# Two FNet and two H3 layers on one core: 16-point groups and rows handed out in three steps, late rows in one region, X sums from an earlier step

## The chip, the core and the metric

The kernel runs on one core of one Trainium2 chip. A core has TensorE (PE, matrix products, with its weight loads shown as PEld), VectorE (DVE), ScalarE (ACT), GpSimd (POOL) and SyncE (SP, which issues most of the transfers). Each engine works through its own queue of instructions in order and waits at an instruction until what that instruction needs is there. The metric is the device time of one execution in microseconds. The kernel before has a median of 1230.15 us over 3 runs (1229.99 to 1231.23).

## What is computed

Two kinds of layer alternate on an array x of 2048 positions and 576 channels, float32 throughout:

```python
x = A_x
x = x + _A_ref(_layernorm(x, axis=-1), A_dft_seq_re, A_dft_seq_im, A_dft_hid_re, A_dft_hid_im)
x = x + _B_ref(_layernorm(x, axis=-1), B_k, B_v, B_shift_k, B_ssm_k, B_ssm_D)
x = x + _A_ref(_layernorm(x, axis=-1), A_dft_seq_re, A_dft_seq_im, A_dft_hid_re, A_dft_hid_im)
x = x + _B_ref(_layernorm(x, axis=-1), B_k, B_v, B_shift_k, B_ssm_k, B_ssm_D)
return x
```

`_A_ref` multiplies by a hidden transform (576 by 576) and a sequence transform (2048 by 2048), both complex, and keeps the real part. `_B_ref(q, k, v, ...)` is q times y, where y is a long convolution (over 2048 positions, for each channel) of kv, and kv is a 4-tap convolution of k times v. k and v are inputs, so y does not depend on x: it is one array, the same for both B layers, and only the gating q * y depends on x.

## The kernel before

**Precision.** Every float32 operand is split into a high part (rounded for fp32r) and a low part: `split(h, l, src)` is an ACT copy (L86) and a DVE subtraction (L87). A product is three matmuls, high by high, high by low, low by high. All matmuls are recorded at L69.

**Rows.** Positions are stored as 16 rows (tiles) of 128 positions, x[:, j, :]; `xs` holds the normalised rows, split. `to_x` (L172 to L178) writes a row there.

**Layer 1 (first A layer).** `layer` (L278) goes through 128 steps n: 4 blocks of 512 output positions (tb), real and imaginary part (g), 16 rows (k). A step loads a c tile of 128 by 512 (`load_c`, two steps ahead; raw tile in the ring `craw`, its split form in the ring `cs`) and does 14 matmuls of 512 columns into four banks s0 to s3 and rm. It yields twice: after half of the sequence matmuls (whole is False) and at its end (whole is True). At the end of a block's part the banks are emptied (`evac_u`, `evac_r`), and four `hidden` products (L254: 54 matmuls of 288 columns each, in two pieces) are put on the list `pending`, to be handed out by `finish` between steps. They use W, the split hidden matrices, loaded by `load_w` (L203) at steps 41 to 43, three chunks each.

**The branch.** y of the B layers is computed beside layer 1 by the generator `branch` (L325): a 128-point transform (`f1_products`, steps up to 40), then 64 groups of 16-point products (`mid_forward`, `mid_inverse`), then the inverse 128-point products (`i2_products`, 32). The main loop (L614 to L646) asks it for its next part whenever a step's share of the time is used up: each part says how much it is worth by what it yields (L508, L514, L524), and `paced` gives each step's share. A group loads a tile of t (`load_feed`, two groups ahead), splits it (`split_feed`, one group ahead), multiplies it (`mid_forward`: two halves of three matmuls each, the kernel half into bank pk, emptied by four ACT copies L434 to L437, and the signal half into px, multiplied by these on DVE, L439 to L441), and two groups later goes back (`mid_inverse`: three matmuls, emptied by L453). All of these, and `hidden`, take their banks in turn from three (`bank`, named bk).

**The gate and layer 2.** `get_x1` (L574) makes row j of the second A layer's input: it loads the first layer's output xa and y's row yb, normalises and gates (`gated`, L526: statistics on DVE, the power on POOL, two passes on DVE), stores xb, normalises again (`normed_x`, L534: two ACT passes with sums, the power on POOL, a third ACT pass), stores the result to y_d and writes it to `xs`. Rows 0 to 7 are made at every second step from step 113 of layer 1 on, rows 8 to 15 at the steps of layer 2 listed in `ROWS`. Their buffers xa and yb are rings of six, two in the tile `flts` and four in the tile `gate`. Layer 2's first block runs 32 steps of `layer`; its sums go out by `save_u` (L708) and `store_r` (L713). At step `STATIC` the regions are laid out anew: rings csum and cw come into `flts`, the tile `ph` into the region that `gate` had. `build_load` (L662) reads pairs of normalised rows back, `build` (L671) forms their sums and differences (four of them, four parts each) for the other three blocks, which `strassen` (L784) computes with seven products in place of eight; its steps load c tiles of twice the size (`raw_c`).

**Order.** The program is written in this order, but each engine's queue is ordered by a scheduler, by its estimate of when an instruction is ready: the trace shows instructions ahead of ones that precede them in the program (L672 of `build`, handed out at step 20, ahead of L717 of step 15). `tc.issue_after(ins)` puts what a block issues on the engine of `ins` behind it; `load_after` keeps SP's loads behind the last c load (`anchor`), `load_fr` those of POOL behind the last power.

Of the kernel before, what the change touches and what calls it, by code (L numbers as in the profile page):

```python
# [27 lines left out]
ROWS = (0, 1, 2, 3, 4, 5, 7, 9)  # L28
# [4 lines left out]
W_SAVE = 60  # L33
I2_END = 111
# [13 lines left out]
STATIC = 14  # L48
B_LOAD = 15
B_FROM = 20  # L50
# [9 lines left out]
def fnet_h3_kernel(ctx: ExitStack, tc: tile.TileContext, x, c_mat, w_re, w_im, k_pad, v, shift_k,  # L60
# [82 lines left out]
    anchor, stored, pows = [], [], []  # L143
# [22 lines left out]
    def normed(src, y):  # L166
        mv, rs, nb = norm_stats(src)
        yield
        nc.vector.tensor_scalar(nb, mv[:, 0:1], rs, -1.0, op0=OP.mult, op1=OP.mult)
        nc.scalar.activation(y, src, AF.Identity, bias=nb, scale=rs)  # L170
# [154 lines left out]
    def branch():  # L325
# [101 lines left out]
        def mid_forward(df):  # L427
            pk, px = bank(), bank()
            for ps, o in ((pk, HD), (px, 0)):
                mm(ps[:, :HD], mc[:, 0, :], df[0][:, o:o + HD], True, False)  # L430
                mm(ps[:, :HD], mc[:, 0, :], df[1][:, o:o + HD], False, False)
                mm(ps[:, :HD], mc[:, 1, :], df[0][:, o:o + HD], False, True)
            kk = two(ring["kk"]())
# [3 lines left out]
            nc.scalar.activation(kk[hi, 1, :], pk[hi, :HD], AF.Copy, scale=-1.0)  # L437
            p1, p2 = kk[:, 0, :], ring["p2"]()
# [62 lines left out]
        for i, (kind, hf, q) in enumerate(feeds):  # L501
# [3 lines left out]
            else:  # L505
# [3 lines left out]
                yfs.append((hf, q, mid_forward(df)))  # L509
# [14 lines left out]
            yield I2_COST if kind else 2.7  # L524

    def gated(xa, j, late=False):  # L526
        mv, rs, _ = norm_stats(xa)
        q = ring["yb"]()
        (load_after if late else nc.sync.dma_start)(q, yb_d[j])
        nc.vector.scalar_tensor_tensor(q, xa, mv[:, 0:1], q, op0=OP.subtract, op1=OP.mult)  # L530
        nc.vector.scalar_tensor_tensor(q, q, rs, xa, op0=OP.mult, op1=OP.add)
        return q

    def normed_x(src, y, junk):  # L534
# [6 lines left out]
        pows.append(nc.gpsimd.tensor_tensor(rs, sv, mhalf, OP.pow).ins)  # L541
        yield
# [16 lines left out]
    def get_x0(j):  # L559
        if X[j] is None:  # L560
            load_x(j + 2)
# [10 lines left out]
    ready = set()  # L572

    def get_x1(j):  # L574
        if j in ready:
            return
        ready.add(j)
        xa = ring["xa"]()
        load_after(xa, xa_d[j])
        xb = gated(xa, j, True)  # L580
        nc.sync.dma_start(xb_d[j], xb)
        y = xa
        for _ in normed_x(xb, y, ring["xj"]()):
            pass
# [29 lines left out]
    for n, whole in layer(get_x0, lambda j: x[:, j, :], done0, pending):  # L614
# [7 lines left out]
        if whole and F1_END < n <= W_END:  # L622
            for _ in range(3):
                next(wl, 0)
            if n == W_END - 1:
                next(br)
# [340 lines left out]
```

## Time and profile before

| what | value |
|---|---|
| median of 3 runs | 1230.15 us (1229.99 to 1231.23) |
| the profiled execution | 1229.91 us |
| its span, first to last instruction | 1228.0 us |
| mean granted TensorE clock | 0.991 |
| DMA | 261.96 MB, mean 213 GB/s |
| shares of the chain that ended last | PE 76%, DVE 7%, DMA 7%, ACT 5%, issue 3% |

How to read it: a line of the busy table gives an engine's busy time, its share of the span and its count of instructions. A row of a timeline gives start, length, engine, line, operation, the tiles written and read, the shape, how many in a row, and in brackets how long the engine stood idle before and what ended that. SPq and ACTq rows are transfers being issued. A row of waits gives who waited for whom, the total, how often, and the longest. The granted clock is the share of full speed that the throttle allowed TensorE.

### The profile page before, as it was taken

The page shows a single profiled execution, that of the slowest core. Times are in us where ns is not written, and L with a number is a line of the kernel's source. Part 1 is how long each engine was busy: PE and PEld are TensorE (multiplying, and loading weights), DVE is VectorE, ACT ScalarE, POOL GpSimd, SP SyncE. Part 2 cuts the span into 40 slices and gives each one's busy share as a digit, 9 for nine tenths or more (in the row PEclk, how much of TensorE's full clock was granted, in tenths as well). Part 3 has the DMA queues.
Part 4 walks back from the last instruction along what each step waited for, and adds up shares of the span by engine and source line. Part 5 has one row for each costly group of instructions (what it writes and reads, how often), then busy time and mean ns, then how long its engine had stood idle before and what let it go on. Part 6 is the DMA issues. An engine that isn't in the chain of part 4 may idle for free.

```text
span 1228.0 us, 18406 instructions
## 1 busy us (share of the span) xinstructions
PE 1189.8 (97%) x6320; PEld 1032.7 (84%) x6320; DVE 849.3 (69%) x1559; ACT 657.3 (54%) x1315; POOL 85.5 (7%) x116
## 2 busy tenths in 40 slices
PE   7999999999999999999999899899999999999997
PEld 5778888887878888888988798788888888889997
DVE  7999982849787567675346864675766767774674
ACT  7855664749776577775445653534444445550210
POOL 2310000000000000000111221000000000000111
PEclk9999999899999999999999899999999999999999
DMA  8889988736655656655976764973474477795631
GB/s 296 302 246 300 313 240 246 218 99 169 210 188 187 220 169 186 202 170 177 316 216 229 259 239 139 282 248 122 130 276 153 145 279 256 248 326 162 214 118 39
DMA packets 145967, 261.96 MB, mean 213 GB/s; under 512 B 15825, under 2 KB 44497, under 8 KB 145874
## 3 DMA queue, kind: packets, MB, share of 16 engines
q1 hardware_dynamic: 102674, 205.73, 52.3%
q10 hardware_dynamic: 36288, 42.48, 9.9%
q0 software_dynamic: 6912, 12.59, 4.1%
q8 instruction: 49, 0.80, 0.3%
q14 instruction: 44, 0.36, 0.1%
HBM read 194.09 MB, written 66.65 MB: 212 GB/s over the span
## 4 chain that ended last, share of the span: by engine, by line
PE 76%; DVE 7%; DMA 7%; ACT 5%; issue 3%; POOL 1%; SPq 0%; ACTq 0%; POOLq 0%; DVEq 0%
PE s L69 41%; PE bk L69 31%; PE rm L69 4%; DVE mats L87 1%; DMA flts<-in_c_mat 1%; DMA f1f<-in_k_pad 1%; DMA gate<-xa 1%; POOL flts L541 1%; ACT mats L86 1%; DMA flts<-in_w_re 1%; ACT flts L436 1%; DVE u L87 1%; DVE flts L160 1%; DMA flts<-t 1%; ACT mid L86 0%
## 5 line engine op out<-in xcount | busy, mean ns | idle before, releaser
L69 PE MATMUL s<-mats 128*128 128x512 f32 x2094 | 530.9, 394 | 11.5 <-DVE u L87 7.7
L69 PEld LDWEIGHTS s<-mats 128*128 128x128 f32 x2094 | 386.3, 189 | 88.0 <-DVE u L87 8.6
L86 ACT ACTIVATE mats<-flts 128x512 fp32r<-128x512 f32 x202 | 126.2, 626 | 106.0 <-PE rm L69 53.8
L87 DVE TENSOR_TENSOR mats<-flts,mats 128x512 fp32r<-128x512 f32 x202 | 138.3, 687 | 53.4 <-ACT mats L86 51.9
L69 PE MATMUL bk<-mid 128*128 128x288 f32 x768 | 128.9, 302 | 7.2 <-ACT mid L86 4.1
L69 PEld LDWEIGHTS bk<-mid 128*128 128x128 f32 x768 | 113.8, 189 | 25.5 <-ACT mid L86 8.4
L87 DVE TENSOR_TENSOR mid<-flts,mid 128x576 fp32r<-128x576 f32 (+1 forms) x160 | 100.5, 637 | 34.9 <-ACT mid L86 29.4
L69 PE MATMUL bk<-w,u 128*128 128x288 f32 x864 | 122.5, 299 | 1.2 <-ACT flts L453 1.2
L69 PEld LDWEIGHTS bk<-w,u 128*128 128x128 f32 x864 | 119.9, 191 | 4.6 <-ACT flts L453 1.6
L86 ACT ACTIVATE mid<-flts 128x576 fp32r<-128x576 f32 (+1 forms) x160 | 92.4, 586 | 37.6 <-DVE flts L442 27.8
L69 PE MATMUL rm<-mats 128*128 128x512 f32 x308 | 96.1, 391 | 3.3 <-DVE flts L717 2.5
L163 POOL TENSOR_TENSOR flts<-flts 128x1 f32<-128x1 f32 x40 | 36.8, 921 | 527.6 <-DVE flts L162 527.6
L69 PEld LDWEIGHTS rm<-mats 128*128 128x128 f32 x308 | 57.5, 188 | 16.3 <-DVE flts L717 2.9
L69 PE MATMUL bk<-f1r 128*128 128x288 f32 x384 | 59.8, 300 | 7.6 <-ACT f1r L86 6.5
L69 PEld LDWEIGHTS bk<-f1r 128*128 128x128 f32 x384 | 56.6, 192 | 11.7 <-ACT f1r L86 6.5
L69 PE MATMUL bk<-mats 128*128 128x288 f32 (+1 forms) x370 | 66.0, 316 | 0.0
L69 PE MATMUL s<-t,mats 128*128 128x512 f32 x258 | 65.6, 396 | 0.0
L265 DVE TENSOR_TENSOR flts<-flts,bk 128x288 f32<-128x288 f32 x48 | 21.6, 451 | 59.3 <-PE bk L69 59.2
L69 PEld LDWEIGHTS s<-t,mats 128*128 128x128 f32 x258 | 49.3, 191 | 10.5
L69 PE MATMUL bk<-mats,t 128*128 128x288 f32 (+1 forms) x362 | 57.4, 302 | 0.0
L69 PEld LDWEIGHTS bk<-mats 128*128 128x128 f32 x370 | 54.4, 188 | 3.2
L399 ACT ACTIVATE flts<-bk 128x288 f32<-128x288 f32 x128 | 48.3, 408 | 14.2 <-PE bk L69 12.2
(145 smaller groups left out, 1542.0 us busy)
## 6 DMA issues: line engine op xcount, KB each, us to landing
flts<-in_c_mat SPq DMA_DIRECT2D x149, 256.0 KB, 3.5
ph<-in_c_mat SPq DMA_DIRECT2D x54, 512.0 KB, 4.6
t<-flts ACTq DMA_DIRECT2D x64, 288.0 KB, 5.0
flts<-t SPq DMA_DIRECT2D x64, 288.0 KB, 3.6
flts<-in_c_mat SPq DMA_DIRECT2D x30, 512.0 KB, 5.0
vd<-flts ACTq DMA_DIRECT2D x64, 144.0 KB, 3.1
flts<-vd SPq DMA_DIRECT2D x32, 288.0 KB, 4.6
mid<-in_i2c POOLq DMA_DIRECT2D x32, 256.0 KB, 4.4
```

The source lines that it names most:

```text
L69: nc.tensor.matmul(ps, lhsT, rhs, start=first, stop=last, skip_group_check=more)
L86: nc.scalar.activation(h, src, AF.Copy)
L87: nc.vector.tensor_tensor(l, src, h.bitcast(F32), OP.subtract)
L160: nc.vector.bn_stats(st[:, i, :], src[:, i * HD:(i + 1) * HD])
L163: pows.append(nc.gpsimd.tensor_tensor(rs, ve, mhalf, OP.pow).ins)
L265: nc.vector.tensor_tensor(r[:, cs], r[:, cs], ps[:, :HD], OP.add)
L399: nc.scalar.activation(so[:, c, :], ps[:, :HD], AF.Copy)
L436: nc.scalar.activation(kk[lo, 1, :], pk[hi, :HD], AF.Copy)
L541: pows.append(nc.gpsimd.tensor_tensor(rs, sv, mhalf, OP.pow).ins)
```

## The change

- `mid_forward` becomes `mid_kernel` (kernel half and its four copies) and `mid_signal` (signal half and what follows). The branch yields 1.6 between them and 1.1 at the end, where it yielded 2.7 at the end.
- The branch's groups are set up at step 44 in place of 42 and handed out from step 45 in place of 44 (`MID_FROM`).
- `get_x1` becomes the generator `make_x1` in three parts: loads and first statistics; gating, store, second sums; normalising, store and split. `advance` moves every row in the making on by one part at each step and starts a new one where there is one. In odd rows the first statistics are sums on ACT (`sums`, two passes over the row) in place of bn_stats on DVE. The load of yb stands ahead of the statistics, also in `done1`.
- Late rows: `ROWS` ends in 6, 8 in place of 7, 9; from step 0 of layer 2 on xa and yb are rings of four, in `gate` alone.
- `STATIC` is step 11 in place of 14. The first `build_load` is at step 12 in place of 15. The parts of `build` are handed out from step 16, one at even and two at odd steps, in place of two at each step from 20 on.
- At the start, row 0's statistics and normalisation come ahead of the first two c tiles in the program, and the DVE instructions of these two are tied behind the row's bias (`biased`); the load of x tile 2 follows the second c tile, as it did.

```diff
 XLEAD = 3
-ROWS = (0, 1, 2, 3, 4, 5, 7, 9)
+ROWS = (0, 1, 2, 3, 4, 5, 6, 8)
 K_FIRST = 2
...
 W_SAVE = 60
+MID_FROM = 45
 I2_END = 111
...
 STAT = 20
-STATIC = 14
-B_LOAD = 15
-B_FROM = 20
+STATIC = 11
+B_FROM = 16
 X_RING = 8
...
-    anchor, stored, pows = [], [], []
+    anchor, stored, pows, biased = [], [], [], []
...
         yield
-        nc.vector.tensor_scalar(nb, mv[:, 0:1], rs, -1.0, op0=OP.mult, op1=OP.mult)
+        biased.append(nc.vector.tensor_scalar(nb, mv[:, 0:1], rs, -1.0, op0=OP.mult, op1=OP.mult).ins)
         nc.scalar.activation(y, src, AF.Identity, bias=nb, scale=rs)
...
-        def mid_forward(df):
-            pk, px = bank(), bank()
-            for ps, o in ((pk, HD), (px, 0)):
-                mm(ps[:, :HD], mc[:, 0, :], df[0][:, o:o + HD], True, False)
-                mm(ps[:, :HD], mc[:, 0, :], df[1][:, o:o + HD], False, False)
-                mm(ps[:, :HD], mc[:, 1, :], df[0][:, o:o + HD], False, True)
-            kk = two(ring["kk"]())
+        def mid_half(df, o):
+            ps = bank()
+            mm(ps[:, :HD], mc[:, 0, :], df[0][:, o:o + HD], True, False)
+            mm(ps[:, :HD], mc[:, 0, :], df[1][:, o:o + HD], False, False)
+            mm(ps[:, :HD], mc[:, 1, :], df[0][:, o:o + HD], False, True)
+            return ps
+        def mid_kernel(df):
+            pk, kk = mid_half(df, HD), two(ring["kk"]())
             nc.scalar.activation(kk[lo, 0, :], pk[lo, :HD], AF.Copy)
...
             nc.scalar.activation(kk[hi, 1, :], pk[hi, :HD], AF.Copy, scale=-1.0)
+            return kk
+        def mid_signal(df, kk):
+            px = mid_half(df, 0)
             p1, p2 = kk[:, 0, :], ring["p2"]()
...
                     yield 0.4
-                yfs.append((hf, q, mid_forward(df)))
+                kk = mid_kernel(df)
+                yield 1.6
+                yfs.append((hf, q, mid_signal(df, kk)))
             split_feed(i + 1)
...
                 load_feed(i + 4)
-            yield I2_COST if kind else 2.7
-
-    def gated(xa, j, late=False):
-        mv, rs, _ = norm_stats(xa)
-        q = ring["yb"]()
-        (load_after if late else nc.sync.dma_start)(q, yb_d[j])
-        nc.vector.scalar_tensor_tensor(q, xa, mv[:, 0:1], q, op0=OP.subtract, op1=OP.mult)
-        nc.vector.scalar_tensor_tensor(q, q, rs, xa, op0=OP.mult, op1=OP.add)
-        return q
-
-    def normed_x(src, y, junk):
+            yield I2_COST if kind else 1.1
+    def sums(src, junk):
         m = ring["stat"]()
...
         pows.append(nc.gpsimd.tensor_tensor(rs, sv, mhalf, OP.pow).ins)
+        return sm, rs, nb
+    def gated(xa, q, j, junk=None):
+        load_after(q, yb_d[j])
+        if junk is None:
+            mv, rs, _ = norm_stats(xa)
+            mean, op = mv[:, 0:1], OP.subtract
+        else:
+            mean, rs, _ = sums(xa, junk)
+            op = OP.add
+        yield
+        nc.vector.scalar_tensor_tensor(q, xa, mean, q, op0=op, op1=OP.mult)
+        nc.vector.scalar_tensor_tensor(q, q, rs, xa, op0=OP.mult, op1=OP.add)
+    def normed_x(src, y, junk):
+        sm, rs, nb = sums(src, junk)
         yield
...
         if X[j] is None:
-            load_x(j + 2)
+            if j > 0:
+                load_x(j + 2)
             stats0(j)
...
-    ready = set()
+    def make_x1(j):
+        xa, q = ring["xa"](), ring["yb"]()
+        load_after(xa, xa_d[j])
+        for _ in gated(xa, q, j, ring["xj"]() if j % 2 else None):
+            yield
+        nc.sync.dma_start(xb_d[j], q)
+        for _ in normed_x(q, xa, ring["xj"]()):
+            yield
+        stored.append(nc.sync.dma_start(y_d[j // 2][:, j % 2, :], xa).ins)
+        X[j] = to_x(xa, j)
+        ready.add(j)
+    ready, making = set(), []
+    def advance(j=None):
+        for row in list(making):
+            if next(row, 0) == 0:
+                making.remove(row)
+        if j is not None:
+            making.append(make_x1(j))
+            next(making[-1])
     def get_x1(j):
-        if j in ready:
-            return
-        ready.add(j)
-        xa = ring["xa"]()
-        load_after(xa, xa_d[j])
-        xb = gated(xa, j, True)
-        nc.sync.dma_start(xb_d[j], xb)
-        y = xa
-        for _ in normed_x(xb, y, ring["xj"]()):
+        assert j in ready
+    def done1(j, xa):
+        q = ring["yb"]()
+        for _ in gated(xa, q, j):
             pass
-        stored.append(nc.sync.dma_start(y_d[j // 2][:, j % 2, :], y).ins)
-        X[j] = to_x(y, j)
-
-    def done1(j, xa):
-        nc.sync.dma_start(out[:, j, :], gated(xa, j, True))
+        nc.sync.dma_start(out[:, j, :], q)
...
     next(br)
-    load_c((0, 0, 0))
-    load_x(1)
-    load_c((0, 0, 1))
     get_x0(0)
+    with tc.issue_after(biased[0]):
+        load_c((0, 0, 0))
+        load_x(1)
+        load_c((0, 0, 1))
+        load_x(2)
     next(br)
...
-    for n in range(W_END + 1, I2_END + 1):
+    for n in range(MID_FROM, I2_END + 1):
         total += STEP + PIECE * pieces(n)
...
                 next(wl, 0)
-            if n == W_END - 1:
-                next(br)
+        if whole and n == MID_FROM - 1:
+            next(br)
         if n > W_END:
...
                 finish(pending, 1)
-            m = n - W_END - 1
-            if m + 1 < len(paced):
+            m = n - MID_FROM
+            if m < 0:
+                done_by = -1.0
+            elif m + 1 < len(paced):
                 done_by = paced[m] + (paced[m + 1] - paced[m] if whole else STEP * 3 / 7)
...
             lay(flts, SC_AT + CRAW * NT + 2 * D, ("xa", D, 2), ("yb", D, 2))
-            lay(region_b(F32, "gate"), 0, ("xa", D, 4), ("yb", D, 4), ("xj", D, 2))
-        if m >= 0 and m % 2 == 0:
-            get_x1(m // 2)
+            gate = region_b(F32, "gate")
+            lay(gate, 0, ("xa", D, 4), ("yb", D, 4), ("xj", D, 2))
+        if m >= 0:
+            advance(None if m % 2 else m // 2)
     T, R, t7 = {}, {}, []
...
         finish(pending, 1)
-        if n in ROWS:
-            get_x1(J // 2 + ROWS.index(n))
+        if n == 0:
+            fresh("xa", "yb")
+            lay(gate, 0, ("xa", D, 4), ("yb", D, 4))
+        advance(J // 2 + ROWS.index(n) if n in ROWS else None)
         if n == STATIC:
...
             ring["cs"].tiles.extend([free, *held])
-        if n >= B_FROM:
-            if (n - B_FROM) % 2 == 0 and len(builds) < KP:
+        if n == STATIC + 1:
+            loaded.append(build_load(0))
+        for _ in range(1 + n % 2 if n >= B_FROM else 0):
+            if next(builds[-1], 0) == 0 if builds else True:
+                if len(builds) == KP:
+                    break
                 builds.append(build(len(builds), *loaded[len(builds)]))
-            next(builds[-1], None)
-            next(builds[-1], None)
-        if n == B_LOAD or n >= B_FROM and (n - B_FROM) % 2 == 0 and len(loaded) < KP:
-            loaded.append(build_load(len(loaded)))
+                next(builds[-1])
+                if len(loaded) < KP:
+                    loaded.append(build_load(len(loaded)))
         if n >= 30:
...
```

## The prediction, made before the changed kernel was run

> **What bounds the kernel now.** I read the head of the page first, then a table of busy time by stage, then the timelines round the stretches where TensorE's column falls short. From the page:
>
> ```profile
> span 1228.0 us, 18406 instructions
> PE 1189.8 (97%) x6320; PEld 1032.7 (84%) x6320; DVE 849.3 (69%) x1559; ACT 657.3 (54%) x1315; POOL 85.5 (7%) x116
> ```
>
> The busy table by stage (stretch, length, busy time and count of PE, weight load, DVE, ACT, POOL, granted clock, DMA share, GB/s):
>
> ```profile
> 200.00:225.00 25.00, 21.59 (x104) 19.02 (x104) 12.93 (x20) 14.32 (x26) 1.58 (x3) 0.86 0.91 289
> 225.00:575.00 350.00, 343.75 (x1936) 299.65 (x1935) 250.57 (x493) 247.39 (x546) 6.75 (x13) 1.00 0.58 178
> 675.00:700.00 25.00, 20.70 (x81) 16.67 (x80) 20.04 (x51) 16.69 (x33) 5.53 (x7) 0.86 0.79 269
> 775.00:800.00 25.00, 21.80 (x87) 16.91 (x86) 19.12 (x35) 13.86 (x26) 0.00 (x0) 0.93 0.93 293
> ```
>
> TensorE sets the time; a change that leaves its matmuls alone can win only its holes. Idle PE (length less busy) is 3.4, 6.3, 4.3 and 3.2 us in these rows, 17.2 of the 38.2 in all (1228.0 less 1189.8); of the rest, the change reaches only the part in term 1. A hole also costs clock: 0.86 over 25 us is 7.0 us at half speed, a loss of 3.5 us on top of the idle; 0.93 is 1.75 us more.
>
> In the stage of the 16-point groups (225 to 575) idle time is not the whole loss. The steady pace is read from two undisturbed pieces of the chain of waits, the work from the groups by shape inside that stretch:
>
> ```profile
> 804.64 2.72 PE s L69 x12
> 1105.63 115.02 PE bk L69 x866
> ```
>
> ```profile
> L69 PE MATMUL s<-mats 128*128 128x512 f32 x697 | 181.9, 393 | 1.6 <-DVE u L87 1.6
> L69 PE MATMUL bk<-mid 128*128 128x288 f32 x636 | 107.8, 301 | 3.8 <-ACT flts L437 1.1 <-ACT flts L453 1.0 <-ACT mid L86 0.7
> L69 PE MATMUL bk<-w,u 128*128 128x288 f32 x487 | 67.0, 295 | 0.0
> L69 PE MATMUL rm<-mats 128*128 128x512 f32 x116 | 36.5, 392 | 0.8 <-ACT flts L464 0.8
> ```
>
> A 512-column matmul takes 2.72/12 = 0.227 us, a 288-column one 115.02/866 = 0.133. (697+116) x 0.227 + (636+487) x 0.133 = 333.9 us, so 16.1 us of the 350 are lost here, the largest sum of any stage, in many small pieces.
>
> **The change part by part.** No matmul is added or removed. The price of each edit is what it does to one hole.
>
> **1. First row's bias first.** The timeline of the start:
>
> ```profile
> 5.10 0.55 POOL L163 TENSOR_TENSOR flts<-flts 128x1 f32<-128x1 f32 x1 [4.66 <-DVE flts L162]
> 6.43 0.76 DVE L87 TENSOR_TENSOR f1r<-f1f,f1r 128x576 fp32r<-128x576 f32 x1 [1.41 <-ACT f1r L86]
> 7.97 0.69 DVE L87 TENSOR_TENSOR mats<-flts,mats 128x512 fp32r<-128x512 f32 x1 [0.77 <-ACT mats L86]
> 9.31 0.20 DVE L169 TENSOR_SCALAR flts<-flts 128x1 f32<-128x1 f32 x1
> 11.33 3.00 PE L69 MATMUL s<-mats 128*128 128x512 f32 x12 [1.55 <-ACT mats L174]
> ```
>
> The bias (L169) could run from 5.65, when the power is done, but stood behind a split of a c tile (7.97). Tied ahead of it, it runs at 7.19 at the latest (behind L87 of 6.43), 2.1 us sooner; the row is then ready before the earlier matmuls end, at 11.33 - 1.55 = 9.8. At most 1.6 us are won. The second row, still as late, is needed next, so I take **1.0**, bounds -0.5 (the c split now waits for the bias) to 1.6. The order of the loads on SP stays: x tile 2 stood behind the second c tile before, too.
>
> **2. The groups start one step later (42/44 to 44/45).** TensorE and SP around the hole:
>
> ```profile
> 212.65 0.39 PE L69 MATMUL s<-mats 128*128 128x512 f32 x1
> 216.45 0.85 PE L69 MATMUL bk<-mid 128*128 128x288 f32 x2 [3.41 <-ACT mid L86]
> ```
>
> ```profile
> 212.35 0.90 SPq L147 DMA_DIRECT2D flts<-t  x2
> 215.65 0.57 SPq L212 DMA_DIRECT2D flts<-in_w_re  x1
> ```
>
> After one matmul of step 44 TensorE waits for the first group, whose two t loads stand in the SP queue among the nine W loads. Later, those loads go behind W, and 13 more matmuls of step 44 (13 x 0.227 = 2.95 us) come before a group is due: they fill nearly all of the 3.41, and the 3.5 of clock goes with it, 6.4 at most. Next late is W: its last tile is issued at 215.65, and the first hidden-size product would now start at 212.65 + 3.2 = 215.9 and want its ninth tile 24 x 0.133 = 3.2 us later, at 219.1. The first group, loaded by the row of 212.35, was ready at 216.45, 4.1 us after its issue; by that measure W's last tile is ready at 219.8, and its split takes its turn behind eight others. The two t loads of 288 KB that no longer stand ahead of it (2 us at the row's 289 GB/s) make up for part of this, so some 2 us of wait and part of the clock may come back. I take **3.0**, bounds -1.5 (t loads now too late: one step's lead instead of two) to 6.4.
>
> **3. Groups in three steps.** A group's nine matmuls were handed out as inverse (3) and forward (6); now inverse, kernel half, signal half, with pauses 0.4 / 1.6 / 1.1 in place of 0.4 / 2.7. What their weight loads waited for between 225 and 575:
>
> ```profile
> PEld bk L69 <- ACT mid L86: 4.4, 11, 0.8
> PEld bk L69 <- ACT flts L437: 4.3, 9, 0.7
> PEld bk L69 <- ACT flts L453: 2.8, 6, 1.2
> PEld bk L69 <- DVE flts L441: 1.4, 4, 0.5
> ```
>
> L437, L453 and L441 empty banks: 8.5 us. With a pause between kernel and signal, the four copies of the kernel half lie under sequence matmuls, and the signal's bank is written only when its factor is ready, so it is held for a shorter time. I take half, **4.0**. L86 (data of the next group late) is untouched or worse, see the rivals. Bounds: the 16.1 of the stage less the hole of the u eviction (1.6) and rm (0.8) that no group causes leaves 13.7; below, -4.4, the L86 row's wait once more. The 64 more changes between kinds of matmul add no instruction.
>
> **4. Rows of layer 2 in three steps; odd rows' first sums on ACT.** DVE and ACT before the hole at 690:
>
> ```profile
> 686.85 0.81 DVE L160 BATCH_NORM_STATS2 flts<-flts 128x6 f32<-128x288 f32 x2
> 688.01 0.81 DVE L530 SCALAR_TENSOR_TENSOR flts<-flts 128x576 f32<-128x576 f32 x1
> 690.06 0.15 DVE L540 TENSOR_SCALAR flts<-flts 128x1 f32<-128x1 f32 x1
> 692.36 0.57 ACT L86 ACTIVATE u<-s 128x512 fp32r<-128x512 f32 x1
> 693.84 1.65 PE L69 MATMUL s<-mats 128*128 128x512 f32 x3 [4.21 <-DVE u L87]
> 688.17 0.76 ACT L539 ACTIVATE gate<-flts 128x576 f32<-128x576 f32 x1
> ```
>
> The layer's first matmul waits for the eviction of s (ACT at 692.36), queued behind row 6's chain, whose L540 (690.06) stands behind row 7's statistics and gating on DVE (from 686.85 on). If only the statistics of row 7, now on ACT, go (0.81 and two short operations), L540 comes about 1.1 us sooner; if its gating (two of 0.81) too falls behind the eviction, 2.7, and with a hole of 1.5 the 3.5 of clock falls too: 6.2. But row 7's operations were brought ahead of an eviction that precedes them in the program, and nothing in the change forbids that; and its two new passes on ACT (0.76 each by the row of L539) may land ahead of the eviction. I take **2.5**, bounds -1.5 to 6.2. Loading q ahead of the statistics in the last rows lies under their matmuls.
>
> **5. Late rows in one region, STATIC 14 to 11, X sums from 16.** The hole near 781 and what precedes it:
>
> ```profile
> 754.33 2.88 PE L69 MATMUL s<-mats 128*128 128x512 f32 x12
> 755.17 0.45 DVE L265 TENSOR_TENSOR flts<-flts,bk 128x288 f32<-128x288 f32 x1
> 768.14 0.33 SPq L585 DMA_DIRECT2D y<-gate  x1
> 768.51 1.20 SPq L147 DMA_DIRECT2D flts<-in_c_mat  x2
> 770.20 2.88 PE L69 MATMUL s<-mats 128*128 128x512 f32 x12
> 771.20 0.63 ACT L86 ACTIVATE t<-flts 128x512 fp32r<-128x512 f32 x1 [1.48 <-DMA flts<-in_c_mat]
> 782.16 0.29 DVE L672 TENSOR_TENSOR flts<-flts 128x128 f32<-128x128 f32 x1 [1.00 <-DMA flts<-y]
> 783.88 0.74 PE L69 MATMUL rm<-mats 128*128 128x512 f32 x2 [2.49 <-DVE flts L717]
> ```
>
> rm waits for store_r's L717, behind X sums (L672) that wait for their y loads. Those loads move from step 15 to 12, about 9.5 us (3 x 3.17, a step from 770.20 - 754.33 over five), and the late rows no longer sit in the flts part that they fill. The sums are then due before the eviction: 2.49 + 1.75 of clock, 4.2 at most. I take **3.5**. Against it: c tiles from step 14 on are now queued on SP behind row 15's store (768.14) and step 14 starts at 770.20; a c tile issued at 768.51 was split from 771.20, plus 0.63: step 14 would stand 1.6 us, with 1.75 of clock 3.4, the lower bound -3.4. Row 15's chain can start up to 3 us sooner (its product ended before 754.33, its L265 came at 755.17, in a DVE queue blocked by row 14's chain), which would hide this.
>
> The Trainium skill ("TensorE: Matmul & The Clock Gate", section "HAM oscillation — how this bites in real kernels") warns only of idle gaps above about 3.4 us; the 2.49 gap here was followed by a clock of 0.93. By that rule term 5 would be 1.75 less than by the row and my sum 1.75 less; the measured clock decides.
>
> **Sum**: 1.0 + 3.0 + 4.0 + 2.5 + 3.5 = 14.0 us off the profiled execution of 1229.91 us (span 1228.0 and 1.9 round it; 0.24 below the median of the runs): **1215.9**. The bounds add to -0.5 - 1.5 - 4.4 - 1.5 - 3.4 = -11.3 (1241.2) and 1.6 + 6.4 + 13.7 + 6.2 + 4.2 = 32.1 (1197.8).
>
> **The rivals.** *A, slower: the next group's data.* split_feed follows the signal half, so its lead on the next kernel half shrinks from 2.7 + 0.4 to 1.1 + 0.4 of a group's 3.1 units, from a full group to half of one, about 2.5 us (350 us over 64 groups and 12 later products is 4.6 us each). The split is an ACT and a DVE pass behind the signal's own operations. It decides once the split ends after its turn on TensorE; at 0.4 us for each of 64 groups it costs 25.6 in place of the gain of 4.0: 1229.9 - 10.0 + 25.6 = 1245.5; at 0.2 us, 1232.7. For it: the L86 row is already the longest. Against: ACT is busy 247 and DVE 251 of 350 us, and the split needs only its load, so it may be brought forward. *B, less: only the late rows act*, and the pace of the groups shifts waits from bank to bank: 1229.9 - 2.5 - 3.5 = 1223.9. *C, more: each hole closes* but for half of the third term's upper bound: 1229.9 - 1.6 - 6.4 - 6.9 - 6.2 - 4.2 = 1204.6. *D, no effect*: each queue is ordered anew, and holes closed open elsewhere: about 1229.
>
> **How the numbers follow.** Forecast (1208 to 1222) 0.48, B (1222 to 1227.7) 0.17, C (below 1208) 0.15, D (within 0.2%, 2.5 us, about what a measurement of this kernel can tell) 0.06, A (above 1232.6) 0.14. Faster is 0.48 + 0.17 + 0.15 = 0.80. The range 1204 to 1232 leaves out half of C and A: about 2 in 10.
>
> **What would show it.** Right: the first sequence matmul by 10; clock 1.00 in 200-225; lost time in the groups' stage near 12 us by the same count; no wait of rm for L717. Wrong: more weight loads waiting for L86 (A); a stall at step 14 of layer 2 with c tiles behind row 15's store; the eviction of s at the layer change still behind row 7 (term 4 nil).

## The result, and the profile after

| kernel | median, us (range, runs) | ratio to before, 95% interval |
|---|---|---|
| before | 1230.15 (1227.54 to 1231.23, 5) | |
| changed | 1237.06 (1235.47 to 1242.35, 5) | 1.0068 (1.004 to 1.0096) |

The change makes the kernel slower, by 0.7%, in the range of rival A; the forecast was 1215.9. The profiled execution of the changed kernel took 1235.47 us, the shortest of its five, and 5.56 more than that of before. From its page:

```profile
PE 1189.6 (96%) x6320; PEld 1030.3 (84%) x6320; DVE 844.1 (68%) x1543; ACT 668.5 (54%) x1347; POOL 79.5 (6%) x116
```

TensorE is as busy as before (1189.8), so it is again a matter of holes. Line numbers are those of each kernel: L434 to L437, L439 to L441, L453 and L464 of before are L436 to L439, L445 to L447, L459 and L470 of the changed kernel, and in some experiments below they are up to three lines off once more (L68 and L85, or L88 and L89, for L69, L86 and L87). The table by stage of the changed kernel, and two rows of before that the prediction did not show:

```profile
200.00:225.00 25.00, 22.02 (x101) 17.75 (x99) 11.50 (x16) 13.48 (x25) 1.58 (x3) 0.93 0.90 278
225.00:575.00 350.00, 343.09 (x1932) 297.59 (x1932) 251.48 (x494) 248.40 (x547) 6.34 (x12) 1.00 0.59 178
575.00:675.00 100.00, 96.46 (x531) 84.94 (x531) 47.55 (x94) 48.43 (x97) 15.70 (x27) 1.00 0.79 249
675.00:700.00 25.00, 18.75 (x78) 14.37 (x77) 17.01 (x43) 18.47 (x41) 4.00 (x7) 0.94 0.75 250
700.00:775.00 75.00, 73.20 (x398) 65.23 (x397) 40.73 (x108) 40.56 (x81) 11.65 (x17) 0.95 0.54 184
775.00:800.00 25.00, 23.27 (x102) 18.90 (x102) 17.65 (x32) 13.22 (x25) 0.00 (x0) 1.00 0.94 316
```

```profile
575.00:675.00 100.00, 98.77 (x541) 86.96 (x541) 49.77 (x100) 47.23 (x92) 15.94 (x27) 1.00 0.81 255
700.00:775.00 75.00, 75.00 (x417) 66.21 (x417) 42.03 (x111) 33.48 (x64) 13.47 (x16) 1.00 0.61 199
```

Idle time plus what the clock lost, stage by stage from before to after: 6.9 to 4.7; 16.1 to 17.5 (the groups, by the prediction's count of lost time, below); 1.2 to 3.5; 7.8 to 7.8; 0 to 5.6; 5.0 to 1.7. The change won 5.5 us in the first and last of these stages and lost 9.3 in the others, 3.8 of the 5.56. The clock column has steps of 0.01, which is 0.25 us in a row of 25 and 1 us in one of 100, and the stretches outside these stages moved too, by 1.2 us or less each; so the balance closes only to about 2 us. The borders between the stages are fixed times: of the 5.6 in 700 to 775, about 1.9 is the slow stretch behind the hole of the layer change, which now runs past 700 (granted clock 0.63 from 700 to 705, 1.00 before).

**The groups** (225 to 575), by shape:

```profile
L69 PE MATMUL s<-mats 128*128 128x512 f32 x689 | 181.2, 392 | 0.1
L69 PE MATMUL bk<-mid 128*128 128x288 f32 x642 | 111.9, 301 | 5.7 <-ACT mid L86 4.1 <-ACT flts L459 0.7 <-ACT flts L439 0.6
L69 PEld LDWEIGHTS bk<-mid 128*128 128x128 f32 x642 | 96.7, 188 | 26.0 <-ACT mid L86 11.2 <-ACT flts L459 2.9 <-ACT flts L439 2.3
L69 PE MATMUL bk<-w,u 128*128 128x288 f32 x486 | 67.1, 295 | 0.6 <-DVE flts L447 0.6
L86 ACT ACTIVATE mid<-flts 128x576 fp32r<-128x576 f32 x76 | 51.7, 682 | 23.6 <-PE bk L69 18.5 <-DMA flts<-t 3.7 <-DMA flts<-vd 0.7
L69 PE MATMUL rm<-mats 128*128 128x512 f32 x115 | 36.0, 391 | 0.4 <-DVE flts L251 0.4
L86 ACT ACTIVATE mid<-flts 128x288 fp32r<-128x288 f32 x63 | 27.8, 441 | 13.9 <-DVE flts L448 13.1
```

Of before, the row of the splits of the groups' data:

```profile
L86 ACT ACTIVATE mid<-flts 128x576 fp32r<-128x576 f32 x75 | 51.1, 682 | 3.5 <-DMA flts<-t 2.0 <-DMA flts<-vd 0.3
```

By the prediction's count, (689 + 115) x 0.227 + (642 + 486) x 0.133 = 332.5 us of work, so 17.5 are lost instead of 16.1. L86 is the line of every split, and two shapes of it write `mid`: 576 wide the data of a group, 288 wide the product that the inverse reads. New is ACT's 18.5 us of idle time ahead of the first, ended by PE. The timeline shows such a wait:

```profile
399.74 1.25 PE L69 MATMUL bk<-mid 128*128 128x288 f32 x8
400.20 0.69 ACT L86 ACTIVATE mid<-flts 128x576 fp32r<-128x576 f32 x1 [3.59 <-PE bk L69]
401.22 0.39 ACT L436 ACTIVATE flts<-bk 64x288 f32<-64x288 f32 x1
402.47 0.41 ACT L439 ACTIVATE flts<-bk 64x288 f32<-64x288 f32 x1
402.90 1.02 ACT L86 ACTIVATE mid<-flts 128x576 fp32r<-128x576 f32 x2
403.95 0.46 DVE L87 TENSOR_TENSOR mid<-flts,mid 128x288 fp32r<-128x288 f32 x1 [0.34 <-ACT mid L86]
403.97 1.07 PE L69 MATMUL bk<-mid 128*128 128x288 f32 x6 [0.31 <-ACT mid L86]
```

The split is queued ahead of the kernel copies (L436 to L439) and waits there 3.59 us for a matmul. The ring `df` has three buffers, so a split that runs two feeds ahead needs the buffer of the feed just used, which now comes free only with that group's signal half. The copies follow late. Behind them, and behind one more split of a group's data, stands the 288-wide split of the earlier group's product (the second of the two at 402.90), and the inverse (403.97) waits for that split, not for a group's data. Taken one by one, all 17 waits of the weight loads for L86 in this stage (11.2 us) end with a 288-wide split.

**After the groups**, the i2 evacuation L470 stands behind a split of data not yet loaded:

```profile
590.78 0.68 ACT L86 ACTIVATE mid<-flts 128x576 fp32r<-128x576 f32 x1 [2.99 <-DMA flts<-vd]
592.31 0.39 ACT L470 ACTIVATE flts<-bk 128x288 f32<-128x288 f32 x1
592.76 1.06 PE L69 MATMUL bk<-mid 128*128 128x288 f32 x6 [3.54 <-ACT flts L470]
```

**The layer change**, where the hole was 4.21:

```profile
691.59 0.78 ACT L539 ACTIVATE gate<-flts 128x576 f32<-128x576 f32 x1 [0.40 <-DVE flts L538]
694.29 0.68 ACT L537 ACTIVATE gate<-flts 128x576 f32<-128x576 f32 x1 [0.54 <-DVE flts L554]
695.72 0.87 ACT L560 ACTIVATE flts<-flts 128x576 f32<-128x576 f32 x1 [0.65 <-DVE flts L559]
697.58 1.06 ACT L86 ACTIVATE u<-s 128x512 fp32r<-128x512 f32 x2
699.22 2.08 PE L69 MATMUL s<-mats 128*128 128x512 f32 x4 [5.17 <-DVE u L87]
```

Row 6's chain (L560) still precedes the eviction (697.58), and of row 7's passes on ACT, L539 (691.59) and a further L537 (694.29) now stand ahead of it too.

**In layer 2** one hole is new and one has moved (L176, a part of the split of a later row's x tile, stands ahead of the bank's reader L265):

```profile
745.92 0.23 DVE L176 TENSOR_TENSOR mats<-gate,mats 128x64 fp32r<-128x64 f32 x1 [1.65 <-ACT mats L174]
746.66 0.45 DVE L265 TENSOR_TENSOR flts<-flts,bk 128x288 f32<-128x288 f32 x1
747.17 5.36 PE L69 MATMUL bk<-w,u 128*128 128x288 f32 x27 [1.80 <-DVE flts L265]
...
780.47 0.69 DVE L711 TENSOR_TENSOR flts<-flts 128x512 f32<-128x512 f32 x1 [2.26 <-DMA flts<-y]
783.33 1.88 PE L69 MATMUL s<-t,mats 128*128 128x512 f32 x7 [1.73 <-ACT t L86]
```

### The profile page after: what moved, and what is told of

Its sections match the earlier page's. It is cut to its first block, busy times and chain, and to the rows that moved or that the text cites. A ratio compares the mean times of both kernels' runs of the same rounds, so it can differ in the third digit from the quotient of the medians.

```text
span 1233.7 us, 18421 instructions
## 1 busy us (share of the span) xinstructions
PE 1189.6 (96%) x6320; PEld 1030.3 (84%) x6320; DVE 844.1 (68%) x1543; ACT 668.5 (54%) x1347; POOL 79.5 (6%) x116
## 4 chain that ended last, share of the span: by engine, by line
PE 75%; DMA 8%; ACT 7%; DVE 5%; issue 3%; POOL 1%; SPq 0%; ACTq 0%; POOLq 0%; DVEq 0%
PE s L69 41%; PE bk L69 30%; PE rm L69 4%; DMA flts<-in_c_mat 1%; ACT mats L86 1%; ACT mid L86 1%; DMA ph<-in_c_mat 1%; DMA flts<-vd 1%; DMA vd<-flts 1%; DVE mats L87 1%; DMA gate<-xa 1%; POOL flts L541 1%; ACT flts L438 1%; DMA t<-ud 1%; ACT flts L439 1%
## 5 line engine op out<-in xcount | busy, mean ns | idle before, releaser
L69 PE MATMUL s<-mats 128*128 128x512 f32 x2088 | 531.3, 394 | 10.3 <-DVE u L87 6.6
L69 PEld LDWEIGHTS s<-mats 128*128 128x128 f32 x2088 | 384.2, 189 | 83.9 <-DVE u L87 8.8
L86 ACT ACTIVATE mats<-flts 128x512 fp32r<-128x512 f32 x199 | 124.5, 627 | 107.3 <-PE rm L69 60.0
L87 DVE TENSOR_TENSOR mats<-flts,mats 128x512 fp32r<-128x512 f32 x199 | 136.6, 688 | 65.7 <-ACT mats L86 63.6
L69 PEld LDWEIGHTS bk<-mid 128*128 128x128 f32 x768 | 114.7, 188 | 30.7 <-ACT mid L86 11.2
L69 PE MATMUL bk<-mid 128*128 128x288 f32 x768 | 131.3, 300 | 9.3 <-ACT mid L86 4.1
L87 DVE TENSOR_TENSOR mid<-flts,mid 128x576 fp32r<-128x576 f32 (+1 forms) x160 | 100.9, 637 | 46.6 <-ACT mid L86 39.8
L69 PE MATMUL bk<-w,u 128*128 128x288 f32 x864 | 124.0, 299 | 5.4 <-ACT w L218 1.9
L69 PEld LDWEIGHTS bk<-w,u 128*128 128x128 f32 x864 | 120.0, 191 | 10.3 <-ACT w L218 2.5
L86 ACT ACTIVATE mid<-flts 128x576 fp32r<-128x576 f32 (+1 forms) x160 | 92.4, 585 | 45.6 <-PE bk L69 18.5
L69 PE MATMUL rm<-mats 128*128 128x512 f32 x304 | 94.3, 390 | 0.4 <-DVE flts L251 0.4
L69 PE MATMUL bk<-f1r 128*128 128x288 f32 x384 | 59.8, 300 | 8.4 <-ACT f1r L86 6.6
L69 PE MATMUL bk<-mats 128*128 128x288 f32 (+1 forms) x376 | 67.8, 317 | 0.0
L69 PEld LDWEIGHTS rm<-mats 128*128 128x128 f32 x304 | 56.9, 188 | 12.7 <-DVE flts L251 0.8
L69 PE MATMUL s<-t,mats 128*128 128x512 f32 x264 | 65.4, 390 | 1.9 <-ACT t L86 1.7
L69 PEld LDWEIGHTS bk<-f1r 128*128 128x128 f32 x384 | 56.6, 192 | 12.6 <-ACT f1r L86 6.6
L163 POOL TENSOR_TENSOR flts<-flts 128x1 f32<-128x1 f32 x32 | 29.7, 927 | 489.5 <-DVE flts L162 488.0
L265 DVE TENSOR_TENSOR flts<-flts,bk 128x288 f32<-128x288 f32 x48 | 21.7, 452 | 57.7 <-PE bk L69 57.6
L69 PEld LDWEIGHTS s<-t,mats 128*128 128x128 f32 x264 | 49.3, 188 | 13.1 <-ACT t L86 2.2
L86 ACT ACTIVATE mats<-ph 128x512 fp32r<-128x512 f32 x54 | 33.6, 628 | 47.8 <-PE bk L69 23.7
L69 PE MATMUL bk<-mats,t 128*128 128x288 f32 (+1 forms) x368 | 59.3, 303 | 0.0
L69 PEld LDWEIGHTS bk<-mats 128*128 128x128 f32 x376 | 55.5, 188 | 3.4
```

The source lines that it names most:

```text
L69: nc.tensor.matmul(ps, lhsT, rhs, start=first, stop=last, skip_group_check=more)
L86: nc.scalar.activation(h, src, AF.Copy)
L87: nc.vector.tensor_tensor(l, src, h.bitcast(F32), OP.subtract)
L163: pows.append(nc.gpsimd.tensor_tensor(rs, ve, mhalf, OP.pow).ins)
L265: nc.vector.tensor_tensor(r[:, cs], r[:, cs], ps[:, :HD], OP.add)
```

## The experiments

Ratios are to runs of the kernel before on the same chip.

**The parts by themselves.** Each is the kernel before with one part of the diff: the three-step groups (`split_alone`), the rows (`rows_alone`), the late rows' region with STATIC and the X sums (`static_alone`), the start from step 44 (`midstart_alone`), the first bias (`bias_alone`).

> The kernel before with the groups' three steps alone. Theory 1 (each part acts in its own place): the stage of the groups, 225 to 575 us, changes by no more than the 0.7 us that it changed by in the changed kernel, the hole near 590 (TensorE waiting 3.5 us for L470) appears because the last groups are handed out otherwise, +3.8 us, and nothing after 700 us differs: 1233 to 1235 in all. Theory 2 (an edit puts every queue behind it in another order): the hole at 590 need not appear, and holes after 640 us change by over 1 us although nothing there was edited.

> The kernel before with layer 2's rows in three steps, odd rows' first sums on ACT and ROWS ending 6, 8. Theory 1: it carries the whole loss after 640 us: the hole at the layer change grows from 4.2 to 5.2 us, with the two small stalls before it +1.6; a new hole of 1.8 us at step 7 of layer 2, TensorE's product waiting for L265 behind row 14's L176, with its clock +3 to 4; the hole at 781 stays: 1235 to 1237. Theory 2: the holes after 640 us are others than in the changed kernel.

> The kernel before with STATIC at 11, the first build_load at 12, the X sums from 16 and the late rows in one region. Theory 1: nothing before 750 us changes, the wait of rm for L717 (2.5 us and its clock) is gone, a wait of 1.7 us for a split behind the sums takes its place without half clock: 4 to 5 us less, 1225 to 1226. Theory 2: the hole at 781 changes, but c tiles queued behind row 15's store open one near step 14 of 2 us and more: 1229 or above.

> The kernel before with the groups set up at step 44 and handed out from 45. Theory 1: the single hole of 3.4 us at 213 breaks up into four waits for W of 0.4 to 1.0 us as in the changed kernel, the lost time of 200 to 225 us stays near 6 us, and nothing else moves by over 1 us: 1229 to 1231. Theory 2: the sum moves by over 2 us through holes after 570 us.

> The kernel before with the first row's bias alone. Theory (term 1): 0.5 to 1.6 us gained at the start, 1227 to 1229, with the rest of the trace as before. Rival (the order of all later instructions moves with it, as in other single edits): anything from 1227 to 1234, the start still about 1 us earlier.

| kernel | median, us | ratio, 95% interval |
|---|---|---|
| split_alone | 1238.57 | 1.0079 (1.0053 to 1.0105) |
| rows_alone | 1231.42 | 1.003 (1.0009 to 1.0052) |
| static_alone | 1230.34 | 1.0014 (0.9996 to 1.0033) |
| midstart_alone | 1231.61 | 1.0027 (1.001 to 1.0045) |
| bias_alone | 1228.64 | 0.9986 (0.9974 to 0.9998) |

The split of the groups costs as much alone as the whole change. Rows and start lose a little, static_alone can't be told from before, and only the bias gains. Of the time ranges of the first theories only the bias's was met; split_alone came out 3.6 us above its range. In its profiled execution, the slowest of its six, the groups' stage loses 21.6 us by the prediction's count, against 17.5 in the changed kernel, so the later start, or another edit of the changed kernel, may take some of the cost of the split away. rows_alone has neither of the two holes that it was expected to bring at their size: 3.77 us at the layer change in place of 5.17, and 0.49 at L265 in place of 1.80. In static_alone the hole at L717 is gone, but two others came:

```profile
767.25 0.32 SPq L584 DMA_DIRECT2D y<-gate  x1
767.63 0.42 SPq L146 DMA_DIRECT2D flts<-in_c_mat  x1
770.60 0.63 ACT L85 ACTIVATE t<-flts 128x512 fp32r<-128x512 f32 x1 [2.65 <-DMA flts<-in_c_mat]
771.28 0.49 PE L68 MATMUL s<-t,mats 128*128 128x512 f32 x1 [1.49 <-ACT t L85]
778.00 2.50 PE L68 MATMUL s<-t,mats 128*128 128x512 f32 x5 [2.75 <-ACT t L85]
```

The c tile behind row 15's store, which the prediction named as term 5's lower bound, costs 1.49 here.

**Is it the lead, or the split at all?** `early_feed` moves, while groups run, the split of the next group between the kernel half and its pause; `no_split` gives the forward out in one piece again, the other edits kept; `lead_before` moves the split ahead of the group's products in the kernel before.

```diff
                 kk = mid_kernel(df)
+                split_feed(i + 1)
+                load_feed(i + 2)
                 yield 1.6
...
-            split_feed(i + 1)
-            load_feed(i + (4 if i > last_mid else 2))
+            if kind:
+                split_feed(i + 1)
+                load_feed(i + (4 if i > last_mid else 2))
```

> The changed kernel with one edit: while groups run, the split of the next group and the load after it stand between the kernel half and its pause of 1.6 units, so the next group's data has 1.6 + 1.1 + 0.4 units of lead again instead of 1.1 + 0.4. Theory (the lead is what the three-step groups lose): between 225 and 575 us the weight loads' wait for L86's mid tiles falls from 11.2 us to 4.4 or less, the hole of 3.5 us near 590 behind a late mid split goes, and the kernel comes out 5 to 8 us below the changed one, 1229 to 1232. Rival (the finer bursts cost by themselves, by waits between bank, factor and signal): L86's wait may fall but the waits for bank evacuations rise, and the time stays within 2 us of 1237.

> The changed kernel with the groups' forward in one hand-out again (pauses 0.4 and 2.7), all other edits kept. Theory (the split is the main loss, and alone it cost 10 us): 1228 to 1231, 6 to 9 us below the changed kernel, with no hole near 590 and L86's wait in the groups' stage near 4.4. Rival (the edits lose by their sum, none by itself: rows 2.8, start 3.0, static 1.8 when each stood alone): 1234 to 1238.

> The kernel before with the split of the next group and the load after it moved ahead of the group's own products, so that the lead grows by the burst itself. Theory (L86's waits are a matter of lead): L86's 4.4 us in the groups' stage falls below 2, time 1 to 3 us below before, 1226 to 1229. Rival (the split then stands in ACT's and DVE's queues ahead of the group's own evacuations): L86's wait falls but waits for L437 and L453 rise by as much or more, 1229 to 1234.

early_feed: 1241.48, 1.0077 (1.005 to 1.0105); no_split: 1232.18, 1.0017 (0.9998 to 1.0036); lead_before: 1231.52, 1.0011 (0.9995 to 1.0028). Without the split most of the loss is gone: the groups' stage loses 15.8 us, and of the 3.54 us ahead of 592.76 a hole of 1.47 stays. The expectation of early_feed failed entirely: L86's wait in the groups is 11.2 us to the digit, and lead_before's moved from 4.4 only to 4.9. The engines' queues are not in program order, so where the split stands in the program was not what made the inverse wait. That led to the buffer and the queue:

**Tie and distance.** `split_tie` ties each 576-wide split behind the kernel copies of an earlier group; `inv_late` puts the inverse between the halves; `both` does both.

```diff
-            split_feed(i + 1)
+            held = copies[-1 if kind else -2:]
+            if held and i < last_mid:
+                with tc.issue_after(held[0]):
+                    split_feed(i + 1)
+            else:
+                split_feed(i + 1)
```

```diff
-                if len(yfs) == MID_LAG:
-                    mid_inverse(*yfs.pop(0))
-                    yield 0.4
                 kk = mid_kernel(df)
-                yield 1.6
+                yield 0.8
+                late_inv = len(yfs) == MID_LAG
+                if late_inv:
+                    mid_inverse(*yfs.pop(0))
+                yield 0.8
                 yfs.append((hf, q, mid_signal(df, kk)))
...
-            yield I2_COST if kind else 1.1
+            yield I2_COST if kind else 1.5 if late_inv else 1.1
```

> The changed kernel with each split of a group's data tied on ACT behind the last kernel copy (L439) of the group before last. Theory (in the changed kernel such a split is queued ahead of those copies and waits there for the signal half that frees its buffer: ACT stood 18.5 us idle before L86 with PE as the releaser, against none before): that idle time falls below 3 us, the weight loads' 11.2 us for L86 fall to about 5, and the time falls by 4 to 7 us, to 1230 to 1233. Rival (ACT's blocked time lies under sequence matmuls, the loss is the shorter way from signal to inverse): ACT's idle time goes, L86's 11.2 stays above 9, time within 2 us of 1237.

> The changed kernel with each group's inverse moved from the group's start to between its kernel and signal halves (pauses 0.8, 0.8, 1.5), so that 5.4 units lie between a signal half and its inverse instead of 4.2 (5.8 before the change). Theory (the 11.2 us are waits of the inverse for its split product, whose way was cut by the pause of 1.6): they fall to about 5, the time by 4 to 7 us, to 1230 to 1233. Rival (ACT's order, not the distance): they stay above 9, time within 2 us of 1237.

> The changed kernel with both edits, the tie of the splits and the later inverse. If the three-step groups lose by these two alone, the groups' stage comes out no slower than before: lost time between 225 and 575 at or below that of before, time 1228 to 1231. If finer bursts cost by themselves, 1234 or more.

The groups' stage, read from the table by shape (lost time by the same count; us):

| kernel | us, ratio (95%) | s + rm, bk | lost | ACT before the 576 split, by PE | weight load for L86 | for L439 |
|---|---|---|---|---|---|---|
| changed | 1237.06, 1.0068 | 804, 1128 | 17.5 | 18.5 | 11.2 | 2.3 |
| split_tie | 1242.77, 1.0094 (1.0064 to 1.0124) | 800, 1123 | 19.0 | 6.8 | 8.2 | 3.0 |
| inv_late | 1236.39, 1.0056 (1.0036 to 1.0077) | 801, 1126 | 18.4 | 13.2 | 3.7 | 11.5 |
| both | 1232.02, 1.0029 (1.001 to 1.0047) | 813, 1128 | 15.4 | 5.9 | 2.8 | 7.3 |

Neither edit alone helps, against both theories: with the tie alone the inverse still waits for its product (8.2); with the later inverse alone that wait goes and one for the kernel copies (11.5) takes its place, because ACT is still held by the splits. (split_tie's time is worse than the changed kernel's because of what lies behind the groups: PE is busy 94.65 of the 100 us to 675 and 68.58 of the 75 from 700.) Together they bring the groups to 15.4, just under before's 16.1, as expected of `both`, with the time a little above the range. So in the changed kernel the cost in this stage lies in these two, and the finer bursts by themselves win next to nothing (no_split, without them, loses 15.8). This holds with the later start of the groups; best1, below, has the earlier one and the same two repairs, and loses more. A fourth buffer in the ring `df` or a third for the product, which would remove the hold itself, was not tried: the region that holds them is full.

**The layer change and the X sums.** `ties` is the kernel before with two orders written out, `ties2` adds row 6 (in `ties` row 7 alone is behind the eviction):

```diff
+            if m == 14:
+                with tc.issue_after(u_out[0]), tc.issue_after(u_out[1]):
+                    get_x1(6)
+                    get_x1(7)
+            elif m != 12:
                 get_x1(m // 2)
...
+            with tc.issue_after(r_out[0]):
                 next(builds[-1], None)
                 next(builds[-1], None)
```

> The kernel before with two orders laid down: row 7's chain behind the last ACT and DVE instruction of the u eviction at the layer change, and the X sums of layer 2 behind store_r's last addition. Theory (the holes of 4.21 at 694 and 2.49 at 781 come from row and sum work hoisted ahead of what TensorE waits for): the first falls below 1.5 without a stretch of half clock, the second goes, 6 to 10 us in all, 1219 to 1224. Rival (closed holes open elsewhere, as in the runs of single parts): row 7 is late at its own step, or the sums crowd the start of the next stage; 1228 to 1232.

> The kernel with the two laid-down orders, with row 6's chain as well as row 7's put behind the u eviction. Theory (the 4.27 us left at 693.65 are the eviction behind row 6's L547 and its X split, 2.9 us of ACT and waits): the hole falls below 1.5 and the clock in 675 to 700 rises from 0.86 to 0.97 or more, 4 to 7 us off 1224.7, 1218 to 1221. Rival (something else holds the eviction, or rows 6 and 7 come late at their own steps): 1223 to 1227.

ties: 1224.73, 0.9956 (0.9938 to 0.9973); ties2: 1221.04, 0.9932 (0.9912 to 0.9951). In ties the second hole went and the first stayed, against its expectation:

```profile
691.96 2.04 ACT L88 ACTIVATE u<-s 128x512 fp32r<-128x512 f32 x4
693.65 1.65 PE L69 MATMUL s<-mats 128*128 128x512 f32 x3 [4.27 <-DVE u L89]
```

In ties2 it closed, and the stage's clock is full:

```profile
687.27 2.05 ACT L88 ACTIVATE u<-s 128x512 fp32r<-128x512 f32 x4
688.74 3.02 PE L69 MATMUL s<-mats 128*128 128x512 f32 x12 [1.47 <-DVE u L89]
...
675.00:700.00 25.00, 23.53 (x120) 19.96 (x119) 18.57 (x45) 13.92 (x27) 4.07 (x5) 1.00 0.71 236
```

Row 6 was what stood ahead of the eviction. `both_tied` puts rows 6 and 7 behind it in the changed kernel with both repairs; `best1` is ties2 with the repaired three-step groups, `best2` that with the bias and the later start too.

> The changed kernel with both repairs of the groups (tie of the splits, later inverse) and rows 6 and 7 of layer 2 started behind the u eviction. The kernel with the two repairs was 1232.0; its hole at the layer change was 5.12 us. Theory (term 4 failed because the chains of rows 6 and 7 are still queued ahead of the eviction): hole below 2, 5 to 8 us less, 1224 to 1227. Rival (the three-step rows lose elsewhere in layer 2, as near 745): 1229 to 1232.

> The kernel before with groups in three steps, the later inverse, the tied splits, and the orders for rows 6 and 7 and the X sums; nothing else of the change. Theory (repaired three-step groups win 2 to 3 us up to 500, and the orders 8): 1216 to 1220, below the 1221.0 of the orders alone. Rival (the groups' gain is lost again by 565, as with the two repairs in the changed kernel): 1220 to 1223.

> The same with the first row's bias first and the groups from step 44 on. Theory (the start wins 1 us, the later groups nothing): 1216 to 1220, within 2 us of the kernel without them. Rival (W, late by its own load, costs its wait when the groups leave: 1 to 3 us more than without): 1220 to 1223.

both_tied: 1229.38, 0.9993 (0.9978 to 1.0009), its hole at the layer change 1.57 us, its time in the range of the rival; best1: 1227.32, 0.998 (0.9969 to 0.9991); best2: 1222.08, 0.9941 (0.9929 to 0.9953). best1 missed both of its ranges, and best2 came out in its rival's. The orders are worth 8 us; what is left of the change adds nothing to them that these runs can tell (ties2 and best2 overlap). best1, without the later start and the first bias, is 5 us above best2. By the count of the table its groups' stage loses 19.9 us (799 and 1118 matmuls) and that of best2 15.9 (811 and 1128), so most of the difference lies there, in one profiled execution of each. Why the repaired groups lose more with the earlier start stays open.

## Why the prediction was wrong

The forecast was 14.0 us less than the profiled execution of before, and the changed kernel's took 5.56 more. By the stages, terms 3 and 4 make most of that: term 3 claimed 4.0, and the groups with what follows them (to 675) lost 3.7; term 4 claimed 2.5, and the stages of the layer change and of layer 2 (675 to 775) lost 5.6.

**Term 3 failed**, at the step "L86 (data of the next group late)". The row mixes two shapes, and what waits is the inverse for its split product. So it was before the change already: all 11 waits of the prediction's row (4.4 us) end with a 288-wide split. So rival A had the right side and place but the wrong carrier: none of these waits ends with a split of the next group's data. (early_feed, meant to lengthen its lead, left the queues nearly as they were, so it says nothing on the lead itself.) Half of the bank waits did not go either. The waits of the changed kernel's weight loads between 225 and 575:

```profile
PEld bk L69 <- ACT mid L86: 11.2, 17, 1.1
PEld bk L69 <- ACT flts L459: 2.9, 6, 1.0
PEld bk L69 <- ACT flts L439: 2.6, 5, 0.7
PEld bk L69 <- DVE flts L447: 1.6, 3, 1.1
```

The three banks make 7.1 us where L437, L453 and L441 made 8.5, a gain of 1.4 for the 4.0 claimed, and L86 took 6.8 back. The prediction never asked which buffer the signal half holds on to, and for how long. Behind the groups the 3.54 at 592.76 came on top, with the clock at 1.00; split_alone has it too (3.64) and no_split a part (1.47), so most of it belongs to this term.

**Term 4** (2.5) failed by its own caveat: "nothing in the change forbids" that row 7 goes ahead of the eviction. The hole grew to 5.17. And the step that said L540 was late because of row 7 looked at the second cause: with row 7 gone (ties) row 6's L540 (L543 there) ran at 688.93 in place of 690.06, as the term had it, but the hole stayed, 4.27; with row 6 gone as well it closed. rows_alone has only 3.77 there, so the growth to 5.17 came with the other edits, in a way that was not found. The row chains also brought the 1.80 at 747.17, which no part of the prediction priced: the same order costs 0.49 in rows_alone, and why it costs more beside the other edits stays open.

**Term 2** (3.0): the single hole turned into waits for W, as foreseen, but in more pieces:

```profile
214.09 1.56 PE L69 MATMUL bk<-w,u 128*128 128x288 f32 x8 [0.66 <-DVE w L87]
216.63 0.40 PE L69 MATMUL bk<-w,u 128*128 128x288 f32 x1 [0.99 <-ACT w L218]
```

With two more waits they make 2.98 us in place of the 3.41, where the prediction took some 2 to come back, and the clock came to 0.93, not to 1.00. The stage won 2.2 us, 1.75 of them by the clock, and that part does not belong to the later start: static_alone, which keeps a hole of 3.46 there, has 0.93 too, and no_split, with the later start, 0.86. So it was luck. midstart_alone wins 2.1 in this stage and is slower all the same (1.0027).

**Term 5** (3.5) was right in mechanism, and in size in the changed kernel: the stage went from 5.0 to 1.7, the clock to 1.00, and L717 no longer holds rm; the X sums took back 1.73 (783.33). That it was no more is partly luck: at the same place stand 2.75 in static_alone, 2.77 in no_split and 2.38 in `both`, and the c tile of step 14 cost 1.49 in static_alone and 0.97 in `both`.

**Term 1** (1.0) fell short too, at the step "it runs at 7.19 at the latest":

```profile
7.98 0.82 DVE L160 BATCH_NORM_STATS2 flts<-early 128x6 f32<-128x288 f32 x2 [0.61 <-DMA early<-in_x]
9.15 0.20 DVE L169 TENSOR_SCALAR flts<-flts 128x1 f32<-128x1 f32 x1
11.18 1.22 PE L69 MATMUL s<-mats 128*128 128x512 f32 x2 [1.23 <-ACT mats L174]
```

The bias (L169) is now ahead of the c tiles, but behind the next row's statistics (L160), which wait for their own load, and it runs at 9.15 where it ran at 9.31. The first sequence matmul starts at 11.18 in place of 11.33, not by 10. In bias_alone the two are at 8.49 and 10.95. That kernel won 0.0026 to 0.0002 of the time, 1.7 us in the middle, but only 0.4 of it at this place.

**The sum** added five gains as if each hole closed for itself. Measured alone, the parts give +9.7, +3.7, +1.7, +3.3 and -1.7 us (ratio less one, times 1230), 16.7 together, against 8.4 of the whole. That they share their holes, and that each edit orders the queues anew elsewhere, would explain it; no run shows how much is due to either.

## What to carry to other kernels

Before a group of work is cut into steps, list what each step keeps (buffers, banks, the place in an engine's queue) until the last one is done: a producer queued ahead on an in-order engine turns that hold into a stall for everything behind it. Read a row of waits by shape before naming its cause, and where a hole comes from work that the compiler moved ahead of an eviction, tie that work behind the eviction; the two ties here brought more than all five parts of the change.

## What the runs showed of the hardware

A hole's length alone did not decide the clock. In the changed kernel, the 1.80 us ahead of 747.17 were followed by a lower clock (27 matmuls in 5.36 us, 0.199 each for 0.133), the 3.54 ahead of 592.76 were not (the clock is the third number from the right):

```profile
590.00:600.00 10.00, 7.24 (x48) 6.78 (x49) 4.02 (x6) 3.68 (x7) 0.53 (x1) 1.00 1.07 379
745.00:755.00 10.00, 8.20 (x41) 7.38 (x40) 4.36 (x11) 1.38 (x3) 0.99 (x1) 0.83 0.46 157
```

In split_alone a hole of the same cause was followed by slow matmuls, 4.22 us for twelve, 0.352 each for 0.227:

```profile
599.24 1.36 PE L69 MATMUL bk<-mid 128*128 128x288 f32 x6 [3.64 <-ACT flts L470]
600.40 4.22 PE L69 MATMUL s<-mats 128*128 128x512 f32 x12
```

The Trainium skill ("TensorE: Matmul & The Clock Gate", section "HAM oscillation — how this bites in real kernels") gives the rule as no idle gaps above about 3.4 us; the 1.80 with a clock of 0.83 differs from it on one side, the 3.54 with a clock of 1.00 on the other, and the 3.64 agrees.
